# Row loads further ahead of their use, and row stores further behind their results, in a hand-ordered attention and projection stage

## The chip, the cores and the metric

One Trainium2 chip; the kernel runs on one of its cores. The metric is device time in microseconds. Five engines work side by side, each down its own list: TensorE (PE, matmuls and transposes; its weight loads are shown as PEld), VectorE (DVE), ScalarE (ACT), GpSimd (POOL) and SyncE (SP), which here does nothing but issue DMAs. A DMA issue that has to wait for a result holds everything behind it in its engine's list. PSUM, where TensorE writes, has eight banks.

## The reference

One sequence of 2048 rows (tokens) of 576 columns passes through an attention block and a mixer block, both behind a conditioned layer norm; all in float32:

```python
mod = (_silu(c) @ w_mod).reshape(c.shape[0], 6, 1, -1)
sa, ca, ga, sb, cb, gb = (mod[:, 0], ..., mod[:, 5])
h = _layernorm(x) * (1 + ca) + sa
x = x + ga * _A_ref(h, A_wqkv, A_wo)      # 32 heads of 18, window of 256 keys, then @ wo
h = _layernorm(x) * (1 + cb) + sb
x = x + gb * _B_ref(h, B_w1, B_w2, B_w3, B_w4)
```

`_B_ref` normalizes again, multiplies by w1 (576 x 576), applies gelu, shifts the four column groups by 1, -1, 2 and -2 rows, multiplies by w2, adds its input, normalizes, and runs a 576 to 4608 to 576 MLP with gelu, added to the sum before.

## The kernel before, in words

The rows are held as 16 blocks of 128 (index t) or four groups of 512 (index g). To keep float32 accuracy, each operand of a large matmul is split into a high and a low part (`split9` does it for a transposed block: TensorE transposes, ScalarE copies the high part, VectorE subtracts), and three products are summed.

The program has these stages:

- query, key and value projections, written out to DRAM (`qkh`, `qkl`) except for the values (about the first 230 us);
- the attention: 32 *units*, each four heads over one group of 512 rows (g outermost, then c, hq). A unit has a load of its queries and keys into one of four U buffers (`uload`, 12 DMAs on SyncE, listed 1.3 units ahead); a pass `s2` for the row maxima (TensorE L477, VectorE L484), which are transposed (L498) and written into the U buffer by a small DMA on ScalarE's queue (`U<-ms`, L501); a pass `s3`, 1.5 units later, with the scores again (L526, L527), the exponential on ScalarE (L533), and the product with the values (L548); and the end, in which the result is transposed (L560), normalized on VectorE (L562, L566) and, for every second unit, stored to `od` (L570, SyncE);
- the output projection `s4(g, i)` for block t = 4g + i, once all eight units of group g are stored. The blocks of groups 0, 1 and 2 (blocks 0 to 11) are played between the attention units of the next groups, one block every two units; the blocks of group 3 belong to the mixer stage;
- the mixer's two small matmuls (`phase_b`), then the MLP (`phase_c`), which fills the second half of the time.

A call of `s4` returns ten steps with their places in the list:

1. `load`: two DMAs on SyncE, the attention's rows (`or<-od`, L741) and the input's rows (`xr<-in_A_x`, L743), each into one of five row buffers (tag "r");
2. `tr`: `split9` of the first into `oT` (TensorE L68 and L72, ScalarE L69 and L73, VectorE L70 and L74);
3. `wo(0)`, `wo(1)`: 14 matmuls each (L761) for half of the columns, and VectorE's addition into `xr` (L762);
4. `put(xp)`: a SyncE store of `xr` (L767);
5. `stat("b")`: the statistics of the rows (VectorE L85 to L87, GpSimd L88 and L89);
6. `ln1`: normalization and modulation in place (VectorE L99 and L101), then `put(hbd)`;
7. `stat("c")`, `ln2`: normalization again in place (VectorE L884), then `put(xnd)`.

Everything of the first stages is put into one list `ev` of (time, step) in units, and `play` calls the steps in order of time. For TensorE, GpSimd and SyncE the order of the list is the order of the program (`manual_schedule`); VectorE's and ScalarE's lists are ordered by the compiler's scheduler from the dependencies, with the list as priority. The step times have no meaning for the clock; they only sort. Waits between engines are added by the compiler from the data.

The tuple `d4` holds, for load, tr, wo(0), wo(1), stat b and stat c, the place within the block, and `l_p = 0.02` is the place of a store behind the step that makes its data (`l_n = 0.05`: of a norm behind its statistics).

Of the kernel before, what the change touches and what calls it, by code (L numbers as in the profile page):

```python
# [50 lines left out]
class Kern:  # L51
# [54 lines left out]
    def row(self, name):  # L106
        return self.rp.tile([P, D], F32, tag="r", name=name, bufs=self.b_row)
# [19 lines left out]
    def phase_a(self):  # L127
# [11 lines left out]
        with ExitStack() as st:  # L139
# [86 lines left out]
            def warm(k):  # L226
                def f():
                    pw = self.ps.tile([P, 512], F32, tag="sc", name=f"pw{k}", bufs=self.b_sc)
                    for _ in range(self.n_warm[k]):
                        nc.tensor.matmul(pw, self.zb, self.zb.unsqueeze(1).to_broadcast([P, 4, P]), start=True, stop=True)  # L230
                return f
# [212 lines left out]
            def uload(c, g, hq):  # L444
                def f():
                    q, k = unit(c, g, hq)
                    h0 = 8 * c + 4 * hq

                    def put(dst, row, src, first, r, c0, c1, eng=nc.sync):
                        v = src[first:first + 4 * DH, c0:c1].rearrange("(j r d) n -> d j r n", r=2, d=DH)[:, :, r, :]  # L450
                        eng.dma_start(dst[row:row + DH].bitcast(F32), v)

                    c0, c1 = max(0, g * 512 - 256), g * 512 + 512
                    kd = k[:, :, 768 - (c1 - c0):]
                    for r in range(2):
                        for n, src in enumerate((qkl, qkh, qkh)):
                            put(kd, 64 * r + n * DH, src, D + h0 * DH, r, c0, c1)
                        for n, src in enumerate((qkh, qkh, qkl)):
                            put(q[:, r::2, :], 64 * r + n * DH, src, h0 * DH, r, g * 512, c1, nc.scalar if c == g == hq == 0 else nc.sync)
                return f  # L460
# [162 lines left out]
            s4 = self.s4  # L623

            def sub2(c, g, hq, tb):
                st, f1, f2 = s2(c, g, hq)
                return [(tb + 0.95 * t / 16, f) for t, f in st] + [(tb + 0.96 + 0.06 * self.lt, f1), (tb + 1.05 + self.l_m, f2)]

            def sub3(c, g, hq, tb):
                st, n, f1, f2, f3 = s3(c, g, hq)  # L630
                e = max(t for t, _ in st) / n * self.ww
                return [(tb + self.ww * t / n, f) for t, f in st] + [(tb + e + self.l_f, f1), (tb + e + self.l_f + self.l_o, f2), (tb + e + self.l_f + self.l_o + self.l_s, f3)]
# [4 lines left out]
            ev = [(T0 - 1.99, lambda: lns[0][0]()), (T0 - 1.98, consts), (T0 - 1.975, cond), (T0 - 1.97, warm(0))]  # L637
# [24 lines left out]
            for kind, a, b in jobs:  # L662
                g = a // 4 if kind == "v" else b
# [14 lines left out]
            for t in range(4, NT):  # L678
                g, i = divmod(t, 4)
                ld, stt, nm, tr = lns[t]  # L680
# [16 lines left out]
            shift = self.t_end + self.u0  # L697

            n = 0
            for g in range(NGA):  # L700
                for c in range(NCH):
                    for hq in range(2):
                        tb = n + shift
                        tu = tb - self.u_ld
                        ev.append((max(tu, ta[n] + 0.01) if n < 4 else tu, uload(c, g, hq)))
                        ev.append((tb - 0.001, lambda c=c, g=g, hq=hq, tb=tb: sub2(c, g, hq, tb)))
                        ev.append((tb + self.o3 - 0.001, lambda c=c, g=g, hq=hq, tb=tb + self.o3: sub3(c, g, hq, tb)))
                        n += 1
                for i in range(4 if g < 3 else 0):
                    t4 = n - 1 + shift + self.o3 + self.ww + self.l_f + self.l_o + self.l_s + self.l_r + 2.0 * i - self.d4[0]  # L710
                    ev += [(t4 + d, f) for d, f in s4(g, i)]
            uw = shift + 2.0
            wb, steps = woload()
            ev.append((uw, wb))
# [12 lines left out]
            for n, (ld, f) in enumerate(steps + w2):  # L727
                d = 0.17 if n < len(steps) else 0.08
# [2 lines left out]
            with self.tc.manual_schedule(engines=self.manual):  # L731
                play(ev)

    def s4(self, g, i):
        nc, rp, row, Wo = self.nc, self.rp, self.row, self.Wo
        t = 4 * g + i
        box = {}

        def load():
            box["o"] = row(f"or{t}")  # L740
            nc.sync.dma_start(box["o"], self.od[g][i * P:(i + 1) * P, :])  # L741
            box["x"] = row(f"xr{t}")
            nc.sync.dma_start(box["x"], self.x[t * P:(t + 1) * P, :])  # L743

        def tr():
            box["T"] = rp.tile([P, 2 * KC + 1, P], F32R, tag="oT", name=f"oT{t}", bufs=1)
            self.split9(box["o"], box["T"], slice(0, P), f"oTT{t}", ("sc", "st") if g < 3 else ("tr", "tr"))

        def wo(hf):
            def f():  # L750
                T, x = box["T"], box["x"]
                cs = slice(hf * 288, (hf + 1) * 288)
                tag = ("sc", "st")[hf] if g < 3 else "mm"
                po = self.ps.tile([P, 288], F32, tag=tag, name=f"po{t}_{hf}", bufs=self.nb[tag])
                pl = []
                for k in range(KC):
                    h, l = Wo["m"][:, k, cs], Wo["m"][:, KC + k, cs]
                    pl += [(T[:, k, :], h), (T[:, k, :], l), (T[:, KC + k, :], h)]
                pl += [(T[:, 2 * KC, :], Wo["h"][:, cs]), (T[:, 2 * KC, :], Wo["l"][:, cs])]
                for n, (l, r) in enumerate(pl):  # L760
                    nc.tensor.matmul(po, l, r, start=(n == 0), stop=(n == len(pl) - 1))  # L761
                nc.vector.tensor_tensor(out=x[:, cs], in0=po, in1=x[:, cs], op=ALU.add)  # L762
            return f

        def put(d):
            def f():
                nc.sync.dma_start(d[t], box["x"])  # L767
            return f

        def stat(k):  # L770
            def f():
                box["s"] = self.stats(box["x"], f"{k}{t}")
            return f

        def ln1():
            x = box["x"]
            self.modulate(x, x, *box["s"], self.cb, self.sb, self.m_s4)

        def ln2():
            x = box["x"]  # L780
            self.norm_t(x, x, *box["s"])
        d = self.d4
        return list(zip(d, (load, tr, wo(0), wo(1)))) + [(d[3] + self.l_p, put(self.xp)), (d[4], stat("b")), (d[4] + self.l_n, ln1), (d[4] + self.l_n + self.l_p, put(self.hbd)), (d[5], stat("c")), (d[5] + self.l_n, ln2), (d[5] + self.l_n + self.l_p, put(self.xnd))]

    def load_w1(self):
        nc, lp = self.nc, self.lp
# [99 lines left out]
    def phase_b(self):  # L886
# [3 lines left out]
        if True:  # L890
# [149 lines left out]

            ev = []
            for i in range(4):
                ev += [(self.e_s4 + self.g_s4 * i + d, f) for d, f in self.s4(3, i)]
            for g in range(NG):
                ev += stage1(g)
                ev += spread(stage2(g), g, g + 0.95)
# [131 lines left out]
    b_o = 1  # L1178
    u0, u_ld = -1.55, 1.3
    e_ld, e_tr, e_w2, e_x1, e_lt, e_s4 = 1.2, 0.7, 1.2, 0.8, 0.8, 0.0  # L1180
    d4 = (-0.2, 0.1, 0.38, 0.56, 0.85, 1.2)
    l_r = 0.5
    t_mv, d_mv = 3.6, 2.3
    c_w, c_t = 8.1, 8.6
# [36 lines left out]
```

## Time and profile before

| | |
|---|---|
| median of 3 runs | 1875.94 us (1875.45 to 1877.85) |
| profiled execution | 1876.79 us |
| its span, first to last instruction | 1875.0 us |
| granted TensorE clock, mean | 0.970 |
| HBM read, written | 107.06 MB, 47.20 MB |
| first and last row load of the projection (`or<-od`) | 324.8 us, 807.9 us |
| DMA busy share, tenths in 40 slices | 6437554333343333553221111111111000000002 |

The span is what the profiler saw of the program; the execution's time has a little before and behind it. A profile row of a timeline reads: start, length, engine, line, operation, what is written and read, count, and in brackets how long the engine was idle before it and what ended that. `SPq` is SyncE issuing a DMA: the length is the issue, not the transfer. Names such as `or<-od` drop the buffer's number. Rows of waits read: engine, tile and line that waited, what ended it, us in total, times, longest.

### The profile page before, as it was taken

Reading aid. Unit: us, or ns where it says so; the run is one execution under the profiler, and the core shown is the slowest. Engines: PE = TensorE matmul, PEld = TensorE weight load, DVE = VectorE, ACT = ScalarE, POOL = GpSimd, SP = SyncE. Lnnn points to the kernel's source line nnn. Section 1 sums busy time; section 2 is a strip of 40 time slices with the busy share of each in tenths; the row PEclk is TensorE's granted clock in tenths of the full one; section 3 lists DMA queues with packets and bytes.
Section 4 is the critical chain, followed back from the end, with each engine's and each line's share of the span. In section 5 each row is a group of like instructions: output and inputs, shape, how many; then the busy total and the mean of one; then the engine's idle time right before and its main releaser. Section 6 shows DMA issues by size and latency. Waiting matters only on the chain.

```text
span 1875.0 us, 30124 instructions
## 1 busy us (share of the span) xinstructions
PE 1750.6 (93%) x11700; PEld 1516.1 (81%) x11700; DVE 976.9 (52%) x2674; ACT 597.4 (32%) x1262; POOL 387.6 (21%) x379
## 2 busy tenths in 40 slices
PE   7999998888778887799999999999999999999999
PEld 5898666666556565699989999999999999999998
DVE  5312577667656665587754444444444444444433
ACT  4622265445444445534421211211211211211211
POOL 4535230000000000021133233332232111111100
PEclk8999999889889899899999999999999999999999
DMA  6437554333343333553221111111111000000002
GB/s 179 146 95 240 180 151 123 109 93 93 106 128 99 93 97 113 150 189 106 82 74 52 34 47 52 40 53 36 44 39 34 27 27 28 27 27 27 1 1 101
DMA packets 97712, 156.89 MB, mean 84 GB/s; under 512 B 11034, under 2 KB 40478, under 8 KB 97570
## 3 DMA queue, kind: packets, MB, share of 16 engines
q1 hardware_dynamic: 86612, 135.12, 24.2%
q10 hardware_dynamic: 10958, 19.85, 3.0%
q8 instruction: 93, 1.52, 0.3%
q14 instruction: 49, 0.40, 0.1%
HBM read 107.06 MB, written 47.20 MB: 82 GB/s over the span
## 4 chain that ended last, share of the span: by engine, by line
PE 77%; DMA 10%; DVE 8%; POOL 2%; ACT 2%; issue 2%; SPq 1%; ACTq 0%; DVEq 0%; POOLq 0%
PE p L1145 24%; PE p L1116 21%; PE pq L422 5%; PE X L526 4%; PE sc L477 3%; PE av L548 3%; PE po L761 3%; DMA or<-od 2%; DVE sc L484 2%; DMA U<-ms 2%; PE X L527 2%; PE pg L957 2%; PE pv L406 2%; PE w L1010 2%; PE p L1118 2%; PE p L1117 2%
## 5 line engine op out<-in xcount | busy, mean ns | idle before, releaser
L1145 PEld LDWEIGHTS p<-CW,Gc 128*128 128x128 f32 x3456 | 474.9, 188 | 16.2 <-DVE Gc L1127 3.7
L1145 PE MATMUL p<-CW,Gc 128*128 128x288 f32 x3456 | 483.2, 295 | 3.4 <-DVE Gc L1127 3.4
L1116 PE MATMUL p<-LNT,CW 128*128 128x512 f32 x1728 | 419.2, 391 | 0.0
L1116 PEld LDWEIGHTS p<-LNT,CW 128*128 128x128 f32 x1728 | 316.3, 188 | 58.8
L1124 ACT ACTIVATE gfc<-p 128x512 f32<-128x512 f32 x144 | 86.2, 599 | 735.5 <-PE p L1118 735.5
L1149 DVE TENSOR_TENSOR acc<-p,acc 128x288 f32<-128x288 f32 x340 | 153.7, 455 | 318.7 <-PE p L1145 315.3
L484 DVE CUSTOM_DVE_ANT_0 sc<-sc,mask 128x384 f32<-128x384 f32 (+2 forms) x512 | 261.1, 553 | 62.5 <-PE sc L477 60.9
L533 ACT ACTIVATE P<-X 128x384 f32<-128x384 f32 x480 | 223.9, 490 | 145.1 <-PE X L527 129.6
L477 PE MATMUL sc<-U 126*128 126x384 f32 (+2 forms) x512 | 202.3, 417 | 10.7 <-DVE m L484 6.8
L526 PE MATMUL X<-U 128*128 128x384 f32 (+2 forms) x704 | 188.0, 327 | 9.7 <-DMA U<-ms 6.0
L526 PEld LDWEIGHTS X<-U 128*128 128x128 f32 x704 | 135.0, 205 | 39.2 <-issue 23.0
L1149 DVE TENSOR_TENSOR accw<-p,accw 128x288 f32<-128x288 f32 x204 | 90.0, 453 | 129.4 <-PE p L1145 128.0
L527 PE MATMUL X<-maskb,identb 128*128 128x256 bf16 x480 | 140.7, 293 | 0.0
L1127 DVE TENSOR_TENSOR Gc<-gfc,Gc 128x512 fp32r<-128x512 f32 x144 | 126.2, 876 | 4.7
L422 PE MATMUL pq<-hT,Wq 128*128 128x512 f32 x504 | 121.2, 397 | 2.4 <-POOL Wq L380 1.6
L477 PEld LDWEIGHTS sc<-U 126*128 126x128 f32 x512 | 101.8, 205 | 19.4 <-DVE m L484 14.8
L422 PEld LDWEIGHTS pq<-hT,Wq 128*128 128x128 f32 x504 | 93.9, 188 | 24.7 <-POOL Wq L380 1.9
L1096 POOL TENSOR_TENSOR CW<-r,CW 128x1024 fp32r<-128x1024 f32 x17 | 41.3, 2427 | 280.5 <-DVE CW L1094 280.5
L548 PE MATMUL av<-P,V 128*32 128x256 f32 (+2 forms) x1472 | 92.1, 379 | 0.0
L1126 ACT CAST Gc<-gfc 128x512 fp32r<-128x512 f32 x144 | 89.5, 621 | 4.6
L1100 POOL TENSOR_TENSOR CW<-r,CW 128x1152 fp32r<-128x1152 f32 x17 | 46.4, 2728 | 157.9 <-DVE CW L1099 157.9
L527 PEld LDWEIGHTS <-identb 128*128 128x128 bf16 x480 | 47.6, 99 | 38.3 <-issue 21.8
(1056 smaller groups left out, 1977.5 us busy)
## 6 DMA issues: line engine op xcount, KB each, us to landing
U<-qkh SPq DMA_DIRECT2D x156, 72.0 KB
U<-qkh SPq DMA_DIRECT2D x96, 108.0 KB
r<-in_B_w_dram SPq DMA_DIRECT2D x18, 576.0 KB
qkh<-hl ACTq DMA_DIRECT2D x36, 256.0 KB
qkl<-hl ACTq DMA_DIRECT2D x36, 256.0 KB
r<-in_B_w_dram SPq DMA_DIRECT2D x18, 512.0 KB
U<-qkl SPq DMA_DIRECT2D x78, 72.0 KB
U<-qkl SPq DMA_DIRECT2D x48, 108.0 KB
```

The costliest lines, as they stand in the source:

```text
L422: nc.tensor.matmul(pq, a, b, start=(n == 0), stop=(n == len(pl) - 1))
L477: nc.tensor.matmul(sc[:, lo:], QZ[:KR, q, i * P:(i + 1) * P], KZ[:KR, j, i * P + lo:(i + 3) * P], start=True, stop=True)
L484: nc.vector.tensor_tensor_reduce(out=sc[:, lo:], in0=sc[:, lo:], in1=mask[:, lo:], scale=1.0, scalar=-3e38, op0=ALU.add, op1=ALU.max, accu ...
L526: nc.tensor.matmul(X[:, x0:x0 + nb, :].rearrange("p a b -> p (a b)"), KZ[:, j, kb * P:(kb + 1) * P], QZ[:, q, qb * P:(qb + nb) * P], start ...
L527: nc.tensor.matmul(X[:, 0::2, :], self.identb, mk, start=False, stop=True)
L533: nc.scalar.activation(Pb[b][:, q, :], Xb[b, q].rearrange("p a b -> p (a b)"), AF.Exp, scale=SCALE)
L548: nc.tensor.matmul(abox[0][32 * q:32 * q + 32, q0:q0 + w], V[4 * g + kb][:, hv:hv + 32], Pb[b][:, q, p0:p0 + w], start=(first and n == 0), ...
L1116: nc.tensor.matmul(pg, W3[:, ws, fs], L[:, xs, :], start=(i == 0), stop=False)
L1126: nc.scalar.copy(Gh, gf)
L1127: nc.vector.tensor_tensor(out=Gl, in0=gf, in1=Gh.bitcast(F32), op=ALU.subtract)
L1145: nc.tensor.matmul(po, a, w, start=(i == 0), stop=(i == len(seq) - 1))
L1149: nc.vector.tensor_tensor(out=acc[t][:, cs], in0=po, in1=acc[t][:, cs], op=ALU.add)
```

## The change

`s4` gets the places as an argument, and their seventh number is the place of a store behind its data. The blocks of groups 0 to 2 use a new tuple `d5`; the blocks of group 3 keep `d4`, with 0.02 as before. `t4` subtracts the tuple's first number, so the row load itself stays where it was in the list, and the steps behind it move.

```diff
                 for i in range(4 if g < 3 else 0):
-                    t4 = n - 1 + shift + self.o3 + self.ww + self.l_f + self.l_o + self.l_s + self.l_r + 2.0 * i - self.d4[0]
-                    ev += [(t4 + d, f) for d, f in s4(g, i)]
+                    t4 = n - 1 + shift + self.o3 + self.ww + self.l_f + self.l_o + self.l_s + self.l_r + 2.0 * i - self.d5[0]
+                    ev += [(t4 + d, f) for d, f in s4(g, i, self.d5)]
...
-    def s4(self, g, i):
+    def s4(self, g, i, d):
...
-        d = self.d4
-        return list(zip(d, (load, tr, wo(0), wo(1)))) + [(d[3] + self.l_p, put(self.xp)), (d[4], stat("b")), (d[4] + self.l_n, ln1), (d[4] + self.l_n + self.l_p, put(self.hbd)), (d[5], stat("c")), (d[5] + self.l_n, ln2), (d[5] + self.l_n + self.l_p, put(self.xnd))]
+        p = d[6]
+        return list(zip(d, (load, tr, wo(0), wo(1)))) + [(d[3] + p, put(self.xp)), (d[4], stat("b")), (d[4] + self.l_n, ln1), (d[4] + self.l_n + p, put(self.hbd)), (d[5], stat("c")), (d[5] + self.l_n, ln2), (d[5] + self.l_n + p, put(self.xnd))]
...
-                ev += [(self.e_s4 + self.g_s4 * i + d, f) for d, f in self.s4(3, i)]
+                ev += [(self.e_s4 + self.g_s4 * i + d, f) for d, f in self.s4(3, i, self.d4)]
...
-    d4 = (-0.2, 0.1, 0.38, 0.56, 0.85, 1.2)
+    d4 = (-0.2, 0.1, 0.38, 0.56, 0.85, 1.2, 0.02)
+    d5 = (-1.1, 0.0, 0.3, 0.5, 1.3, 2.3, 0.55)
```

## The prediction

> **What bounds the kernel now.** I read the page from the top: busy times, the forty slices, the chain.
>
> ```profile
> PE 1750.6 (93%) x11700; PEld 1516.1 (81%) x11700; DVE 976.9 (52%) x2674; ACT 597.4 (32%) x1262; POOL 387.6 (21%) x379
> PE   7999998888778887799999999999999999999999
> DVE  5312577667656665587754444444444444444433
> PEclk8999999889889899899999999999999999999999
> PE 77%; DMA 10%; DVE 8%; POOL 2%; ACT 2%; issue 2%; SPq 1%; ACTq 0%; DVEq 0%; POOLq 0%
> ```
>
> TensorE is the bound over the whole, but slices 7 to 16 (328 to 797 us) show 7s and 8s and a reduced clock. That is the attention, with blocks 0 to 11 of the output projection in between. The second view is busy time by stretch: attention alone, attention with projection, one pair of units, the attention's end, the start of the mixer.
>
> ```profile
> 259.90:279.70 19.80, 19.20 (x186) 14.07 (x186) 15.92 (x73) 12.74 (x28) 7.20 (x7) 1.00 0.46 140
> 313.10:716.20 403.10, 327.21 (x2688) 248.79 (x2687) 255.14 (x889) 184.91 (x401) 15.79 (x40) 0.90 0.36 105
> 423.80:461.80 38.00, 31.58 (x259) 24.20 (x258) 24.58 (x86) 17.56 (x38) 1.58 (x4) 0.91 0.37 107
> 716.20:762.20 46.00, 41.19 (x353) 29.75 (x351) 27.23 (x96) 26.61 (x69) 2.37 (x6) 0.99 0.29 91
> 762.20:850.00 87.80, 74.22 (x545) 71.24 (x546) 65.11 (x183) 35.53 (x96) 12.80 (x25) 0.90 0.57 179
> ```
>
> The columns are length, then busy time (and count) of PE, PEld, DVE, ACT, POOL, then granted clock, DMA share and GB/s. In the 403.10 us from 313.1 to 716.2 (21 units, from one unit's first head transpose to another's) PE is busy 327.21: idle 75.9, at a clock of 0.90. Before the projection starts, two units took 19.80 us with PE idle 0.6, at full clock. So this stretch loses time to something particular. The idle time in it, by the tile that waited (first and last of the sorted waits, and the sum of the eleven):
>
> ```profile
> PE oTT8pa L68 <- DMA or<-od: 8.2, 1, 8.2
> PE oTT10pa L68 <- DMA or<-od: 5.3, 1, 5.3
>   DMA or<-od: 65.4, 11
> ```
>
> 65.4 of the 75.9 us is the first transpose of blocks 0 to 10, waiting for the load of the attention output's rows. Block 3, seen from SyncE's queue and from TensorE and VectorE:
>
> ```profile
> 417.28 0.34 SPq L767 DMA_DIRECT2D xp<-xr  x1
> 429.04 0.34 SPq L767 DMA_DIRECT2D hbd<-xr  x1
> 429.47 0.30 SPq L451 DMA_DIRECT2D U<-qkl  x1
> 435.53 0.32 SPq L451 DMA_DIRECT2D U<-qkl  x1
> 435.94 0.34 SPq L767 DMA_DIRECT2D xnd<-xr  x1
> 436.81 0.56 SPq L741 DMA_DIRECT2D or<-od  x1
> 441.88 1.09 PE L68 MATMUL oTT3pa<-ident,or 128*128 128x128 f32 x4 [5.79 <-DMA or<-od]
> 414.65 1.84 PE L761 MATMUL po<-Wom,oT 128*128 128x288 f32 x12
> 428.19 0.81 DVE L101 SCALAR_TENSOR_TENSOR xr<-xr,b2rs,sb 128x576 f32<-128x576 f32 x1
> 431.80 0.58 DVE L884 TENSOR_SCALAR xr<-xr,c2mv,c2rs 128x576 f32<-128x576 f32 x1
> ```
>
> SyncE works strictly down its list. It stood at block 2's store to hbd until L101 ended at 429.0, although the next item, the U loads of a coming unit, could have gone earlier. Those took it from 429.47 to 435.85; then came xnd, od and only at 436.81 the row load for block 3. TensorE had reached the transposes at 441.88 - 5.79 = 436.09. So the load is issued 0.7 us after it is needed, and lands about 5 us later. Over the stretch these stores hold the queue longest:
>
> ```profile
> SPq L767 <- DVE xr L101: 113.4, 10, 11.4
> SPq L767 <- DVE xr L762: 80.9, 10, 9.1
> ```
>
> The clock falls with each such wait. The eleven windows at half clock in the stretch (first, one with a long wait, last, and the sum):
>
> ```profile
> 327.90:331.30 3.40, 3.40 (x17) 0.50 0.57 151
> 631.70:641.90 10.20, 4.43 (x21) 0.50 0.53 162
> 710.20:717.00 6.80, 3.84 (x18) 0.50 0.40 131
> sum 82.10, PE 50.73; mean PE 4.61
> ```
>
> PE was busy 50.73 us in them, at half speed: at full clock that is 25.4 us of work, so 25.4 us is lost beside the waiting itself.
>
> **The change part by part.** Counts stay: per block two loads, three stores, five transposes, 28 matmuls, the same VectorE and GpSimd work. Only list places move, in units of the attention (one unit is 403.10 / 21 = 19.2 us now), counted from the row load, which stays at n - 1 + 3.32 units.
>
> Row loads to transposes: from 0.3 to 1.1 units. Projection halves: from 0.58 and 0.76 to 1.4 and 1.6. Stores: xp from 0.78 to 2.15, hbd from 1.12 to 3.0, xnd from 1.47 to 4.0. VectorE's list is not written by hand, but its inputs move: first statistics from 1.05 to 2.4, second from 1.4 to 3.4; GpSimd's rs steps, two per statistics, move with them. Its queue is busy 15.79 of 403.10 us there, so they cost nothing unless VectorE waits.
>
> *Transposes later.* Between load and transposes stand 0.8 units more of TensorE work. Even at 14 us a unit that is 11.2 us; the longest wait is 8.2. So even if SyncE were no earlier than now, no transpose would wait: 65.4 us goes. I take all of it. Bounds: 0 if SyncE is held longer than today, 65.4 at most.
>
> *Clock.* Without waits of 3.4 to 8.2 us the half-clock windows should not occur: the units before 313 show none (1.00). I take 25.4. If idle pieces of another kind replaced the waits, up to all of it stays; bounds 0 and 25.4.
>
> The Trainium skill, TensorE: Matmul & The Clock Gate, Part 1, says that about 3.4 us of sustained work restores the full clock after an idle window. By that alone at most 3.4 us of half-speed work follows each wait, 11 x 1.7 = 18.7 us lost, an estimate that would give 1797. The trace does not quite agree: 50.73 / 11 = 4.6 us of busy time at half clock per wait, and I keep the trace's figure.
>
> *Stores later.* xp, hbd and xnd stand 0.55 units after the VectorE step that makes their data, not 0.02. In block 2 L101 was listed 1.20 units before block 3's transposes and ran at 428.2, 7.9 us before TensorE got there; at 14 to 19 us a unit that is 0.4 to 0.56 units, so L101 came 0.64 to 0.8 units late. With 0.55 SyncE should still wait for it, but 0.1 to 0.25 units (1.4 to 3.5 us) instead of up to 11.4, and the U loads start about when their buffer is free. I count no further gain, since U loads hardly hold TensorE here. Each store is moved past the next one or two loads and a U set on SyncE; 0.35 us of issue each, the same number as before. What is queued behind them are U loads with over a unit of slack.
>
> *Buffers.* A row xr now lives 4.0 units instead of 1.5. Alive at most: or and xr of one block, xr of two before it, four of five r buffers. The xnd store of block i falls level with the load of block i + 2, but its ln2 is listed 0.55 units before. Cost nothing; if a load did wait there, 1.1 units (15 us) still hide it.
>
> *In-place updates.* L99 overwrites xr and must wait until the xp store has read it; L884 must wait for hbd. The gaps in the list are 0.30 and 0.45 units (before: 0.32 and 0.33), which at 14 us a unit are 4.2 and 6.3 us. Today they cost little:
>
> ```profile
> DVE xr L884 <- DMA hbd<-xr: 0.4, 1, 0.4
> 794.17 3.67 DMA xp<-xr
> 833.17 4.63 DMA xp<-xr
> ```
>
> The first row is all the waiting of this kind in the stretch; the other two, of the chain, are what one store costs where VectorE arrives at once. I take nothing, with bounds of nothing and one landing of 4.6 us per update.
>
> *What is late next.* Without waits the stretch is 403.1 - 65.4 - 25.4 = 312.3 us, 14.9 per unit. It keeps the other 10.5 us of idle time, 3.4%. VectorE's 255.14 us would be 82% of it. In 259.9 to 279.7 VectorE was busy 80% and TensorE idle 3%, so this is a density that the kernel has shown. If the 10.5 went too, 302 us; VectorE's work would come more even (statistics and norm no longer pile up in one unit), which speaks for it, but I leave it in the range.
>
> *The end.* Block 11's transposes go from 32.62 to 33.42 and its halves to 33.72 and 33.92, level with or behind the last head transposes (33.72). 4.8 us of TensorE work (1.09 of transposes, two halves of 1.84) and about 6 us of VectorE work (a split of 0.69 and a tail, two adds of 0.46, four statistics of 0.46, L99 like L101 0.81, L884 0.58) land in the start of the mixer. There TensorE waits anyway, the last two rows:
>
> ```profile
> L70 DVE TENSOR_TENSOR oT<-oTT0pa,oT x1: 692/692/692, 329.0 to 329.0; 128x512 fp32r<-128x512 f32 x1
> L762 DVE TENSOR_TENSOR xr<-po,xr 128x288 f32<-128x288 f32 x20 | 9.2, 458 | 35.4 <-PE po L761 34.6 <-DMA U<-qkl 0.8
> L85 DVE BATCH_NORM_STATS2 b1st<-xr x1: 461/461/461, 372.7 to 372.7; 128x6 f32<-128x288 f32 x1
> 765.53 1.09 PE L1055 MATMUL xnT0pa<-ident,xn 128*128 128x128 f32 x4 [2.65 <-issue]
> 772.71 1.12 PE L1055 MATMUL xnT1pa<-ident,xn 128*128 128x128 f32 x4 [5.88 <-DVE T L912]
> ```
>
> Against that, SyncE's weight loads there are no longer held by block 11's stores. Bounds: 5 us gained (holds gone) to 11 lost (all of it exposed). I take 4 lost, since the second wait is on VectorE already.
>
> **Sum.** The profiled execution took 1876.79 us, span 1875.0; the median of the runs, 1875.94, is 0.05% lower and I ignore that. 1876.8 - 65.4 - 25.4 + 4 = 1790.0.
>
> **The rivals.**
>
> *A new small wait each unit takes back part.* Two candidates: the row maxima's little load (U<-ms), on which the first score matmul of each unit depends, and VectorE's in-place waits.
>
> ```profile
> 396.47 0.47 PE L526 MATMUL X<-U 128*128 128x128 f32 x2 [1.44 <-DMA U<-ms]
> PE X L526 <- DMA U<-ms: 2.7, 3, 1.3
> ```
>
> The first row is the longest in the stretch, the second the attention before it. From its transposes to its use the list gives 0.35 units, 6.7 us now and 4.9 at 14. If all 21 units waited 1.44 us: 30 us back, 1820. Against it: the U loads would be issued before that moment, not into it as at 429 to 436.
> The Trainium skill, DMA: Bandwidth & Descriptors, Issuing engines are not separate DMA queues, says that transfers of SyncE and ScalarE interleave on the same 16 engines. That speaks against this change, since hbd and xnd now stand 0.17 units behind these transposes. No run so far shows such a meeting in the new order.
>
> *Slower: VectorE waits for stores.* Place: L99 behind xp, L884 behind hbd, with the coming units' maxima queued behind on VectorE and TensorE stopped after three score banks (some 1.5 us). If each waits w, a block loses 2 (w - 1.5), and 2 x 2.3 by the clock, against 90.8 / 11 = 8.25 gained. It decides from w = 3.3 us. At w = 4.6, the landing above, 2 x 3.1 + 4.6 - 8.25 = 2.5 per block: 11 x 2.5 = 28 us and the end's 4, 1909. Against it: SyncE is less held, so stores leave early enough.
>
> *It doesn't do what it says.* If SyncE, held by xnd or od, issued the row loads more than 11 us later than today, the waits stay: 1877. For it only that xnd stands level with the load; against it, the 0.55 units of lead.
>
> **How the numbers follow.** The forecast (waits and clock recovered, no new wait over 15 us in sum) has 0.65, and lies from 1771 (the other idle 10.5 gone, 9 us better at the end) to 1808. The partial return has 0.25, 1808 to 1850. The same within 0.2% (3.8 us, what a measurement can tell) 0.03, slower 0.05, odds between 0.02. 1770 to 1832 leaves out slower, same, and the upper part of the partial return. Faster 0.92, same 0.03, slower 0.05.
>
> **What would show it.** Right: no wait for or<-od at L68 in blocks 0 to 10; full clock from 313 us to the mixer; the stretch of 21 units near 312 us; the waits of L767 for L101 and L762 mostly gone. Wrong: waits of L99 or L884 for stores, of L526 for U<-ms in every unit, or half-clock windows that persist; or a mixer start that is later by more than 11 us after the last head transpose.

## The result, and the profile after

The changed kernel takes 1772.47 us (median of 4 runs, 1771.97 to 1773.79) against 1875.7 us: a ratio of 0.9451, 95% interval 0.9434 to 0.9467. The forecast was 1790; the kernel is faster by 103 us where 87 were expected, close to the fast end of the forecast's range (1771 to 1808). The profiled execution took 1772.65 us, its span 1770.4.

The same lines of the page as before the change:

```profile
PE 1722.6 (97%) x11700; PEld 1493.0 (84%) x11700; DVE 976.2 (55%) x2674; ACT 594.3 (34%) x1262; POOL 389.7 (22%) x379
PE   7999999999999989999999999999999999999999
DVE  5412378788888866977544444444444444444434
PEclk8999999999999999999999999999999999999999
PE 55%; DVE 2%; POOL 1%; issue 0%; DMA 0%; SPq 0%; ACT 0%; ACTq 0%; DVEq 0%; POOLq 0%
```

TensorE's row and its clock are now flat through the attention. VectorE's work is the same 976 us, packed closer: 8s where 6s and 7s stood. DMA, 10% of the chain before, is gone from it.

Busy time by stretch, changed kernel: 21 units between the same two head transposes, the next three units, and the rest; last, the rest of the kernel before.

```profile
313.10:618.20 305.10, 299.66 (x2683) 226.69 (x2682) 252.13 (x881) 180.56 (x398) 15.06 (x38) 1.00 0.46 134
618.20:662.60 44.40, 38.98 (x331) 27.70 (x329) 28.25 (x100) 28.20 (x75) 2.67 (x6) 0.92 0.38 117
662.60:1770.40 1107.80, 1091.52 (x6804) 1003.82 (x6804) 548.17 (x1209) 254.21 (x495) 250.66 (x169) 1.00 0.18 55
762.20:1875.00 1112.80, 1090.45 (x6776) 1003.03 (x6776) 547.21 (x1204) 254.51 (x498) 248.24 (x167) 0.99 0.17 54
```

The first 313.1 us are the same. The stretch fell from 403.1 to 305.1, by 98.0: TensorE's idle time from 75.9 to 5.4 (70.5), its busy time from 327.2 to 299.7 (27.5) with the same matmuls, at a clock of 1.00 instead of 0.90. The last three units and the rest fell by 1.6 and 5.0. That is all of the 104.6 us between the spans.

Besides the waits for rows, the stretch held idle time of other kinds. The largest waits of these kinds, before (three rows; ten waits like the third add up to 2.8 us) and after (two rows):

```profile
PE sc L477 <- DVE m L484: 3.8, 10, 0.8
PE X L526 <- DMA U<-ms: 3.3, 5, 1.4
PE sc L477 <- DVE c1mv L87: 0.3, 1, 0.3
PE sc L477 <- DVE m L484: 2.7, 7, 0.5
PE oTT4pa L68 <- DVE m L484: 0.8, 1, 0.8
```

Block 3 again, SyncE's row load and TensorE's transposes, and what held SyncE (313 to 640 us):

```profile
410.12 0.45 SPq L741 DMA_DIRECT2D or<-od  x1
420.54 0.66 PE L68 MATMUL oTT3pa<-ident,or 128*128 128x128 f32 x4
SPq L451 <- DMA U<-ms: 121.7, 21, 8.9
SPq L767 <- DVE xr L101: 7.2, 1, 7.2
```

The load goes out 10.4 us ahead of the transposes, not 0.7 us after TensorE stood at them, and nothing waits. SyncE's 113.4 us at the hbd stores have become 7.2; it now stands at the U loads instead (put down to U<-ms), for which TensorE waits once, 0.5 us. It looks as if freeing SyncE of the stores had been worth a good part. What it was worth, the experiments have to tell.

### The profile page after: what moved, and what is told of

The parts are those of the page before. It is cut to its first block, busy times and chain, and to the rows that moved or that the text cites. A ratio compares the mean times of both kernels' runs of the same rounds, so it can differ in the third digit from the quotient of the medians.

```text
span 1770.4 us, 30143 instructions
## 1 busy us (share of the span) xinstructions
PE 1722.6 (97%) x11700; PEld 1493.0 (84%) x11700; DVE 976.2 (55%) x2674; ACT 594.3 (34%) x1262; POOL 389.7 (22%) x379
## 4 chain that ended last, share of the span: by engine, by line
PE 55%; DVE 2%; POOL 1%; issue 0%; DMA 0%; SPq 0%; ACT 0%; ACTq 0%; DVEq 0%; POOLq 0%
PE p L1145 26%; PE p L1116 22%; PE p L1118 2%; PE p L1117 2%; PE w L1010 2%; PE pg L957 2%; DVE x L1011 0%; DVE G L975 0%; DVE G L962 0%; DVE LNT L70 0%; DMA r<-in_B_w_dram 0%; POOL CW L1100 0%; DVE xm L884 0%; DVE CW L1095 0%; DVE Gc L1127 0%
## 5 line engine op out<-in xcount | busy, mean ns | idle before, releaser
L1149 DVE TENSOR_TENSOR acc<-p,acc 128x288 f32<-128x288 f32 x340 | 154.1, 456 | 319.6 <-PE p L1145 316.2
L477 PE MATMUL sc<-U 126*128 126x384 f32 (+2 forms) x512 | 195.3, 403 | 7.3 <-DVE m L484 5.6
L526 PE MATMUL X<-U 128*128 128x384 f32 (+2 forms) x704 | 180.8, 316 | 5.9 <-DMA U<-ms 3.2
L526 PEld LDWEIGHTS X<-U 128*128 128x128 f32 x704 | 127.2, 193 | 34.6 <-issue 24.5
L527 PE MATMUL X<-maskb,identb 128*128 128x256 bf16 x480 | 136.6, 285 | 0.0
L477 PEld LDWEIGHTS sc<-U 126*128 126x128 f32 x512 | 97.7, 197 | 14.3 <-DVE m L484 10.9
```

What stands on the lines that cost most here:

```text
L477: nc.tensor.matmul(sc[:, lo:], QZ[:KR, q, i * P:(i + 1) * P], KZ[:KR, j, i * P + lo:(i + 3) * P], start=True, stop=True)
L526: nc.tensor.matmul(X[:, x0:x0 + nb, :].rearrange("p a b -> p (a b)"), KZ[:, j, kb * P:(kb + 1) * P], QZ[:, q, qb * P:(qb + nb) * P], start ...
L527: nc.tensor.matmul(X[:, 0::2, :], self.identb, mk, start=False, stop=True)
L1149: nc.vector.tensor_tensor(out=acc[t][:, cs], in0=po, in1=acc[t][:, cs], op=ALU.add)
```

## The experiments

My theory: the row loads' lead over the transposes is what counts, and the clock follows the waits. The rival: the stores behind their results free SyncE, without which the loads stay late. Ratios are to the kernel before, run beside each.

**The lead alone.** From the changed kernel:

```diff
-    d5 = (-1.1, 0.0, 0.3, 0.5, 1.3, 2.3, 0.55)
+    d5 = (-1.1, 0.0, 0.28, 0.46, 0.75, 1.1, 0.02)
```

> The row loads alone are moved: blocks 0 to 11 use the old places (stores 0.02 behind their results) with the load 0.8 units further ahead of the rest (1.1 before the transposes). Theory A (the lead alone removes the waits: TensorE has 0.8 units, 11 us, of other work where it waited 5 to 8): no wait for or<-od at the transposes, full clock in the stretch, 1770 to 1785 us. Theory B (SyncE must also be freed of the stores, else the loads stay late or the U loads of the units do): waits of 2 us and more remain in most blocks, at the transposes or at L526, 1800 us or more.

1790.35 us, ratio 0.9533 (0.951 to 0.9555): 87 to 89 of the 103 us, a little slower than theory A allowed. The stretch, TensorE's longest wait for rows, one of the waits for the second statistics, and SyncE's list around the load of block 4:

```profile
311.50:627.70 316.20, 299.61 (x2684) 226.97 (x2683) 248.17 (x881) 182.31 (x399) 15.05 (x38) 1.00 0.44 131
PE oTT8pa L68 <- DMA or<-od: 1.4, 1, 1.4
PE sc L477 <- DVE c8mv L87: 0.9, 1, 0.9
450.12 0.33 SPq L767 DMA_DIRECT2D hbd<-xr  x1
450.54 0.38 SPq L741 DMA_DIRECT2D or<-od  x1
```

The clock is full and the busy time is that of the changed kernel. But 16.6 us of idle time stay, where the changed kernel has 5.4: the load still follows the hbd store, which stood until its data was ready, and goes out only some 3 us ahead. So theory A holds for most of the gain, and something of the other half is worth 11 us in the stretch; another 6.5 us are lost behind it (45.9 us for the three units, 1112.8 for the rest).

**The other half alone**: loads, transposes and halves at the old places, statistics and stores as far behind the halves as in the changed kernel.

```diff
-    d5 = (-1.1, 0.0, 0.3, 0.5, 1.3, 2.3, 0.55)
+    d5 = (-0.2, 0.1, 0.38, 0.56, 1.36, 2.36, 0.55)
```

> The other half alone: loads, transposes and projection halves at the old places (0.3 units from load to transposes), statistics and stores as far behind the second half as in the changed kernel (0.8, 1.8, stores 0.55 behind). Theory A: in the changed kernel the load goes out 10 us ahead of the transposes, and 0.8 units are 11.8 us, so here it would still go out 1 to 2 us after TensorE stands at them; waits of 5 us and half clock remain, 1850 to 1876 us. Theory B (the stores held the queue): the load goes out in time, waits under 2 us, 1775 to 1800 us.

1841.25 us, 0.9803 (0.9755 to 0.9852): 37 us faster than before, between the theories and nearer to A. The stretch, the longest and the shortest wait for rows, and the sum of the half-clock windows in it:

```profile
313.90:678.80 364.90, 319.90 (x2689) 245.22 (x2689) 254.08 (x888) 181.72 (x401) 15.84 (x40) 0.93 0.39 116
PE oTT2pa L68 <- DMA or<-od: 5.0, 1, 5.0
PE oTT5pa L68 <- DMA or<-od: 2.8, 1, 2.8
sum 51.60, PE 42.61; mean PE 3.87
```

The waits remain, only shorter, and with them the half clock. In 8 of the 11 blocks the row load goes out about 1 us ahead of TensorE's arrival at the transposes (theory A had 1 to 2 us after it; in the kernel before it was 0.5 us or more after it in every block), but its rows take up to 5.9 us to land. So the other half is worth 37 us on the old lead and 15 to 18 us on top of the new one, 11 of them in the stretch: the two halves overlap, and their gains don't add. This run also checks how I priced the clock: half of 42.61 is 21.3 us, and the busy time stands 20.2 above the changed kernel's 299.7.

**The waits filled.** Into the kernel before (its later lines move down by three):

```diff
+        if tags[0] == "sc":
+            for _ in range(14 if name == "oTT0" else 22):
+                nc.tensor.matmul(pa.rearrange("p a b -> p (a b)"), self.zb, self.zb.unsqueeze(1).to_broadcast([P, 4, P]), start=True, stop=True)
         for k in range(KC):
             nc.tensor.transpose(pa[:, k, :], row[:, k * P:(k + 1) * P], self.ident)
```

> The kernel before with idle TensorE time filled: in front of the transposes of blocks 1 to 11 stand 22 matmuls of a zero tile (bf16, 128x512, at full clock about 0.21 us each, 4.7 us), 14 for block 0, into the PSUM tile that the transposes then overwrite. The load's landing doesn't move. If the half clock comes of the idle wait, its 25 us come back although the waits for the rows stay: about 1850 us, half-clock time in the stretch under 20 us of 82. If the half clock has another cause (the transposes, the load itself), no gain or a loss: 1875 to 1885 us.

1872.06 us, 0.9967 (0.9948 to 0.9986): a gain, but 6 us and not 25. The stretch; the added matmuls in it; the wait left at block 3:

```profile
316.00:707.50 391.50, 363.29 (x2923) 255.79 (x2921) 251.94 (x887) 182.64 (x400) 15.85 (x40) 0.98 0.37 109
316.00:707.50 391.50, 52.43 (x234) 22.04 (x234) 0.98 0.37 109
PE oTT3pa L71 <- DMA or<-od: 1.0, 1, 1.0
```

The clock went from 0.90 to 0.98, and half clock is left in two places only, some 14 us in sum instead of 82: behind the two waits for rows that stayed over 3 us, at blocks 4 and 8. The others are at most 1.2 us, and the clock there is full. So the half clock does come of the idle waits.

```profile
PE oTT8pa L71 <- DMA or<-od: 3.4, 1, 3.4
PE oTT4pa L71 <- DMA or<-od: 3.3, 1, 3.3
```

TensorE's own busy time fell from 327.2 to 363.3 - 52.4 = 310.9, by 16.3 us, but the stretch only by 11.7. TensorE now also waits for VectorE (4.9 us up to 640 us at the projection halves, none before), and the three units behind the stretch took 49.4 us instead of 46.0. So with the waits for rows in place, the stretch got back somewhat less than half of the clock's 25.4 us. The added matmuls also hold one of the three score banks for longer; how much of the rest is due to that, and how much to the two windows that are left, stays open.

**Block 11 at its old places**, the rest as changed:

```diff
+                    d5 = self.d4 if 4 * g + i == 11 else self.d5
...
```

(the next two lines then use `d5` in place of `self.d5`)

> The changed kernel, but block 11 (the last one before the mixer) at the old places. The changed kernel took 44.4 us for the last three units and 1107.8 us from there on, against 46.0 and 1112.8 before: 6.6 us gained where I had forecast 4 lost. Theory C (block 11's stores no longer stand in front of the mixer's weight loads on SyncE): these 5 to 7 us are lost again, about 1778 us. Theory D (the start of the mixer gains because the earlier blocks are done sooner, or block 11 has nothing to do with it): within 2 us of the changed kernel, 1772 us, or faster by the 4 us of exposed work I had forecast, 1768 us.

1778.71 us, 0.9474 (0.9451 to 0.9497): the stretch is the same (304.9), but 5.9 us are lost from there on, as much as theory C had it. The interval overlaps that of the changed kernel, but the profile of a second run of the changed kernel has the same 1107.8 us for the rest, and here it is 1112.5. From SyncE's list before the mixer, with two of the waits, and the mixer's first and second transposes (in this kernel, later lines are one higher):

```profile
653.36 0.33 SPq L804 DMA_DIRECT2D rw<-in_B_w_dram  x1
660.32 0.33 SPq L768 DMA_DIRECT2D xp<-xr  x1
660.74 0.48 SPq L77 DMA_DIRECT2D rw<-in_B_w_dram  x1
SPq L768 <- DVE xr L763: 6.5, 1, 6.5
669.89 0.43 SPq L570 DMA_DIRECT2D od<-o  x1
ACT T L912 <- DMA od<-o: 1.8, 1, 1.8
667.90 1.08 PE L1056 MATMUL xnT0pa<-ident,xn 128*128 128x128 f32 x4 [2.92 <-issue]
674.82 1.11 PE L1056 MATMUL xnT1pa<-ident,xn 128*128 128x128 f32 x4 [5.62 <-DVE T L913]
```

and in the changed kernel:

```profile
653.55 0.33 SPq L803 DMA_DIRECT2D rw<-in_B_w_dram  x1
656.29 0.48 SPq L77 DMA_DIRECT2D rw<-in_B_w_dram  x1
665.81 0.44 SPq L570 DMA_DIRECT2D od<-o  x1
664.98 1.76 PE L761 MATMUL po<-Wom,oT 128*128 128x288 f32 x12
667.56 0.66 PE L1055 MATMUL xnT0pa<-ident,xn 128*128 128x128 f32 x4 [0.55 <-DVE xr L762]
670.08 1.11 PE L1055 MATMUL xnT1pa<-ident,xn 128*128 128x128 f32 x4 [1.76 <-DVE T L912]
```

TensorE's two waits are 8.5 us here and 2.3 us in the changed kernel, and that is the loss. Two things differ. Block 11's xp store, waiting 6.5 us for the second projection half, stands in front of the mixer's weight loads; without it the next weight load goes out 4 us sooner. The second wait, put down to VectorE, goes back over ScalarE's copy (L912) to the last store of the attention (`od<-o`), which stands behind these loads on SyncE: it is issued 5.6 us after the last head transposes here, 3.2 us in the changed kernel. And in the changed kernel block 11's projection halves run from 663.1 to 667.0 us, behind the last head transposes (662.6), where TensorE has nothing to do here. So the loss is as large as theory C had it and lies where it put it, but how the 5.9 us divide between the store and the halves, this run does not tell.

**All stores close again**, statistics left where the change put them:

```diff
-    d5 = (-1.1, 0.0, 0.3, 0.5, 1.3, 2.3, 0.55)
+    d5 = (-1.1, 0.0, 0.3, 0.5, 1.3, 2.3, 0.02)
```

> The changed kernel with the stores again 0.02 behind their results; loads, transposes, halves and statistics stay at the new places. The lead alone (statistics and stores both at the old distances) left 316.2 us for the stretch of 21 units, the whole change 305.1. Theory S (the 11 us are the store delay: a store that waits for VectorE holds the U loads and the next row load): stretch of 313 us or more, load issued about 3.5 us ahead of the transposes, about 1786 to 1792 us. Theory T (they are the statistics moved further behind the halves): stretch within 3 us of 305, about 1773 to 1777 us.

1772.37 us, 0.9443 (0.9421 to 0.9464): no difference from the changed kernel. Stretch, three units, rest:

```profile
312.00:616.40 304.40, 301.33 (x2685) 227.29 (x2684) 252.14 (x881) 181.82 (x399) 14.99 (x38) 1.00 0.46 135
616.40:657.10 40.70, 38.00 (x331) 26.37 (x329) 28.02 (x97) 27.37 (x71) 2.43 (x6) 1.00 0.40 127
657.10:1770.40 1113.30, 1093.72 (x6804) 1006.65 (x6804) 549.42 (x1211) 254.20 (x498) 249.20 (x169) 0.99 0.17 54
```

Theory S falls. The 0.55 units buy nothing in the stretch; what the lead alone lacked is the later statistics. They also carry the hbd store past the next row load: in the list it stands 1.92 units behind its block's load in the run with the lead alone, just ahead of the next load at 2.0, and at 2.47 here. SyncE hardly stands at the hbd stores in this run either (5.6 us up to 640 us), so the later statistics suffice to end the 113.4 us, and the run does not say what that wait was worth. The next one says more.

**The load still earlier**, statistics old: the lead-alone kernel with the row load 0.4 units up and nothing else moved.

```diff
-                    t4 = n - 1 + ... + 2.0 * i - self.d5[0]
+                    t4 = n - 1 + ... + 2.0 * i + 1.1
...
-    d5 = (-1.1, 0.0, 0.3, 0.5, 1.3, 2.3, 0.55)
+    d5 = (-1.5, 0.0, 0.28, 0.46, 0.75, 1.1, 0.02)
```

> As the run with the row loads alone moved (old statistics, stores 0.02 behind), with the row load another 0.4 units earlier in SyncE's list and every other step where it was. That run kept 0.6 to 1.4 us of waiting for or<-od at the transposes of blocks 1 to 10 (some 9 us) and 0.9 us per block at a score matmul behind VectorE's second statistics (some 9 us). If the load's place is what is left of the first: no wait for or<-od, stretch near 308 us instead of 316, about 1781 us. If the stores before it hold SyncE anyway: no change, 1790 us.

1781.36 us, 0.9491 (0.9474 to 0.9508). The stretch, and a wait of the kind that is left:

```profile
312.70:622.70 310.00, 300.87 (x2684) 228.26 (x2683) 247.99 (x881) 182.13 (x399) 15.02 (x38) 1.00 0.45 133
PE sc L477 <- DVE c8mv L87: 1.0, 1, 1.0
SPq L767 <- DVE xr L101: 65.1, 10, 6.9
```

No transpose waits for rows. So of the 11 us between 316.2 and 305.1, 6 were the load behind the hbd store, and the remaining 5 came with the statistics: score matmuls stand behind VectorE's second statistics, which the changed kernel avoids. The last row (313 to 640 us) shows what a wait at the stores is worth: SyncE still stands 65.1 us at the hbd stores, but now behind the row load, and no transpose waits. The wait for the stores costs what stands behind it, and little by itself.

**A shorter lead**: 0.7 units, later steps 0.4 earlier.

```diff
+    d5 = (-0.7, 0.0, 0.3, 0.5, 1.3, 2.3, 0.55)
```

> The changed kernel with 0.7 instead of 1.1 units from the row load to the transposes; all later steps move up by 0.4 units. In the changed kernel the load went out 10.3 us ahead of the transposes in most blocks and needs about 4.5 to 5 us; 0.4 units are 5.9 us, so about 4.4 us are left: waits of up to 1 us per block, full clock, 1772 to 1782 us if the lead alone counts. If SyncE's place in its list shifts with the earlier stores so that the load goes out late again: waits over 2 us, half-clock windows, 1790 us or more.

1786.12 us, 0.9514 (0.9489 to 0.954), worse than expected.

```profile
315.90:632.30 316.40, 302.75 (x2684) 228.07 (x2683) 248.39 (x881) 183.14 (x399) 15.05 (x38) 0.99 0.44 129
PE oTT10pa L68 <- DMA or<-od: 1.4, 1, 1.4
PE X L526 <- DVE oT L74: 3.7, 9, 0.4
```

The waits for rows are about as short as forecast (up to 1.4 us), but transposes and halves now fall into one unit; units take 18.2 and 12.3 us by turns (15.5 and 13.9 in the changed kernel), with new small waits for VectorE. So the place within a unit seems to count beside the lead; I had left that out, and no run moves the place alone.

**Stores 0.75 behind**, only 0.10 units ahead of the norm that overwrites their rows:

```diff
+    d5 = (-1.1, 0.0, 0.3, 0.5, 1.3, 2.3, 0.75)
```

> The changed kernel with the stores 0.75 instead of 0.55 units behind their results, so that the xp store stands only 0.10 units (1.5 us) ahead of the norm that overwrites its rows, and the hbd store 0.25 units ahead of the second norm. Rival of the prediction (VectorE waits for stores before its in-place norms): L99 waits 1 to 4 us for xp in most blocks and TensorE's score matmuls for VectorE; 1785 to 1830 us. Otherwise VectorE runs late enough by itself: no such waits over 0.5 us and 1770 to 1776 us.

1778.64 us, 0.9478 (0.9456 to 0.9499). VectorE waited for no store in the stretch, which took 304.3 us: the prediction's slower rival is not there even with most of its margin gone. The 6 us were lost behind it, in one wait of the last unit and a mixer start as slow as before the change:

```profile
655.22 0.69 PE L526 MATMUL X<-U 128*128 128x256 f32 x2 [3.70 <-ACT P L533]
665.60:1778.20 1112.60, 1093.68 (x6804) 1005.70 (x6804) 548.13 (x1208) 253.42 (x495) 251.27 (x169) 0.99 0.17 54
```

**The same for blocks 12 to 15**, in the mixer:

```diff
-    d4 = (-0.2, 0.1, 0.38, 0.56, 0.85, 1.2, 0.02)
+    d4 = (-0.6, 0.1, 0.38, 0.56, 0.85, 1.2, 0.2)
```

> The changed kernel with the same idea for blocks 12 to 15 in the mixer: row loads 0.6 instead of 0.2 units ahead of the block's place, stores 0.2 instead of 0.02 units behind. In the changed kernel TensorE waited there in single pieces of at most 1.8 us, none of them for a row load, so no gain is expected: 1770 to 1775 us. If the order of SyncE's list in the mixer's start still costs: up to 6 us less, 1766 us; if the list places disturb the weight loads: over 1776 us.

1780.61 us, 0.9489 (0.9468 to 0.9509): slower than the changed kernel. Its time behind the last head transposes is 1114.6 us, not 1107.8, and a block's transposes there wait 2.23 us for VectorE, none for rows. A lead where no load is late brought nothing here and seems to disturb the order; single executions of the changed kernel lie between 1772.0 and 1779.6 us (see the next run), so the 7 to 8 us are about as much as that spread.

**Far stores for block 11 alone**, and the changed kernel again beside it:

```diff
-        p = d[6]
+        p = d[6] if t >= 11 else 0.02
```

> The changed kernel with the stores 0.02 behind their results in blocks 0 to 10 and 0.55 behind in block 11 alone. With all stores close the three units after the stretch took 40.7 us (44.4 in the changed kernel) and the rest 1113.3 (1107.8), the same total. If the two ends come of different stores (the units' end of blocks 9 and 10, the mixer's start of block 11), both gains are had: 304 + 41 + 1108, about 1767 us. If they are one thing moved about: 1772 us as the changed kernel.

> The changed kernel once more, beside the run with far stores in block 11 alone, so that both stand against the same runs of the kernel before: 1771 to 1774 us.

1776.08 and 1774.37 us, ratios 0.9461 (0.9444 to 0.9479) and 0.9461 (0.9441 to 0.9481): the same. The two ends did not add up:

```profile
616.40:659.10 42.70, 38.11 (x331) 26.40 (x330) 27.90 (x97) 27.36 (x71) 2.44 (x6) 1.00 0.39 121
659.10:1769.30 1110.20, 1090.29 (x6804) 1002.19 (x6804) 547.83 (x1211) 254.77 (x498) 249.97 (x169) 1.00 0.18 54
```

42.7 and 1110.2 us lie between the two kernels (44.4 and 1107.8; 40.7 and 1113.3). The profiled execution of this kernel, 1771.2 us, was its fastest. No version beat the changed kernel.

## Why the prediction was right, and where not

- *Transposes later* (65.4 us): right in full. The claim that they would not wait even if SyncE were no earlier was a little too strong: with the lead alone 8.2 us were left in sum, up to 1.4 at a block, because the hbd store stands just ahead of the next load.
- *Clock* (25.4): right in size; the busy time fell by 27.5, and the shorter waits of the second run give 20.2 for 21.3. But it is not a term on its own: with the waits filled and nearly full clock, 11.7 us came back in the stretch.
- *Stores later* (nothing): right in size, by the run with close stores. The path was not: SyncE's 113.4 us at the hbd stores went with the stores 0.02 behind their results, too (5.6 left); it is enough that the statistics, and the stores with them, come later. Nor was that wait harmless as such: in the kernel before it held the row load of block 3, and on the old lead later statistics and stores were worth 37 us. Once the row load stands ahead of the store, 65.1 us of it can stay without a late row.
- *Other idle time* (10.5 kept): mis-sized, 5.4 measured. The later statistics, which I named and left in the range, took the waits for the second statistics away (2.8 us); the 3.3 us of waits for U<-ms went, too, and no run says why. With the busy time 2.1 us lower than the clock term had it, the stretch was 305.1, not 312.3: 7.2 us of the miss.
- *The end* (4 lost): the step that failed. 6.6 us were gained, more than the bound of 5. I took block 11's work as exposed and as the larger side, the freed weight loads as the smaller. But its projection halves ran where TensorE had waited, between the last head transposes and the mixer's first, and the wait at the second fell from 5.88 to 1.76 us; with block 11 at its old places 5.9 us were lost again. That is 10.6 us of the miss. (The 1.09 us that I priced the transposes at is a row at half clock; at full clock they take 0.66.) The gain hangs on the order there: with the lead alone, the stores 0.75 behind or the other lead for blocks 12 to 15, everything behind the stretch took 1158.6 to 1159.2 us, as in the kernel before (1158.8), not 1152.2.
- *In-place updates* (nothing): right, and right with a third of the margin for xp and about half of it for hbd.
- *A new small wait each unit*: not there; U<-ms held no matmul of the stretch, although hbd and xnd stand close behind its transposes. The Trainium skill, DMA: Bandwidth & Descriptors, Issuing engines are not separate DMA queues, says that such transfers interleave on the same 16 engines; the changed kernel's stretch shows no cost of that. One pause of 1.44 us put down to U<-ms came behind the stretch, as long as the longest in the stretch before.

## What to carry to other kernels

In a list that one engine works off in order, ask of each load not how far ahead of its use it is listed, but what stands directly in front of it and when that can go: here a store waiting for VectorE. More work between load and use cured nearly all of the late load here, whatever held it; try that first, alone, and look at each other part of the change by itself. A wait in such a list (113 us of SyncE) is worth what stands behind it: with the row load moved ahead, 65 us of it stayed and held no transpose. And the pause of a matmul engine costs more than its length when the clock falls with it, but in this kernel less than half of that share came back when the pause was filled instead of removed.

## What was not expected of the hardware

The kernel before has half clock behind waits of 3.4 us and more, but shorter pauses went with it, too. In the second run, a pause of 2.8 us at one transpose was followed by a half-clock window of 3.4 us. In the changed kernel a pause of 1.44 us, which ended at 647.7 us, was followed by half clock from 649.5 to 656.4 us; a second pause of 1.63 us lies inside that window. Yet a single pause of 1.33 us at 248 us had none, and in the run with the lead alone neither had one of 2.68 us, which ended at 661.7 us. So the length of the pause alone does not decide; what does, the runs do not show.
